# Threshold attention and a gated feed-forward on one core: second pair's transposes, value loads and weight loads moved later in the opening slots, idle transposes added on TensorE

## The chip, the cores and the metric

The kernel runs on one core of one Trainium2 chip. The metric is the device time of a whole execution in microseconds (us). Six runs of the kernel before gave a median of 565.81 us (563.64 to 567.03). A further execution was recorded by the hardware profiler; every duration of a single instruction below comes from that one.

## The reference

Two stages, for 8 batches of 8 heads with 576 positions of 64 values each:

```python
# stage 1, for every batch and head
scores = q @ k.T / 8
thresh = max(scores, axis=-1) - tau                # tau = 0.02
scores = where(scores >= thresh, scores, -1e9)
attn   = exp(scores - max(scores))
attn   = attn / (sum(attn) + 1e-9)
y      = attn @ v
# stage 2; x is y with heads side by side: 4608 tokens of 512
h   = x @ w_in                                     # 512 -> 2048
g   = h * clip(h + 3, 0, 6) / 6
out = g @ w_out                                    # 2048 -> 512, float32
```

## The kernel before

**Units of work.** A *pair* is two heads of a batch; a *quad* is two pairs. There are 16 quads, two for each batch. For each quad the main loop (L439) runs 9 *slots*, 144 in all; n counts them from 0. Slots 0 to 3 of a quad are the four blocks of 128 query rows of its first pair, slots 4 to 7 those of its second pair, and slot 8 takes the last 64 rows of all four heads. Each slot is two tiles (one per head) of 128 rows by 576 keys.

**A slot's softmax** runs over four engines. TensorE (PE) computes the scores into PSUM (`scores`, L251); VectorE (DVE) copies each tile to SBUF and takes the row maximum (`sm_max`, L271); GpSimd (POOL) turns the maximum into a bias (L281); ScalarE (ACT) masks by the threshold (`sm_mask`, L284) and, one slot later, exponentiates (`sm_exp`, L289); DVE inverts the row sums (L293); POOL scales and writes bf16 (`sm_norm`, L296). The result must then be transposed. In most slots SP issues a DMA transpose (L307). In every second slot of the first `N1` = 22 (the flag `on_chip`, L434) PE does it two slots later with nine transposes into the one buffer of pool `ps_h` (`pe_transpose`, L310), and DVE copies it out (L316).

**Inputs.** `load_quad` (L80) makes five load jobs for a quad: keys of the first pair, queries of the first pair, the 64 left-over rows, keys of the second pair, queries of the second pair. Each job is two DMAs from SP (queries of the last batches are four). `load_v` makes four POOL DMAs per batch, `load_weights` sixteen for `w_in` and sixteen for `w_out`, also from POOL, which casts them to bf16 on the way. `start(jobs, n)` issues the next n jobs of a list; the loop does this at the end of every slot (L515 to L517). q and k must be transposed before use: `transpose_q`, `transpose_k` (four PE transposes of 128x128 each, L214, then one copy) and `transpose_rest` (L229).

**Order.** The program is in the order in which it is written: each engine runs its own instructions strictly in this order and waits for the others by semaphores. So an instruction that waits holds back all that stands behind it on its engine. `scores` for slot n+1 are issued at the end of slot n (L510), after the transposes of slot n. The pool of score tiles `ps_s` has two buffers, so the scores of slot n+1 wait for `sm_max` of slot n. `ps_h` has one buffer: the on-chip transposes and the hidden layer of stage 2 (`mm1`, L349) take turns in it.

**Opening.** Five load jobs of quad 0 are issued, fourteen idle transposes of the identity (`warm_up`, L163) run on PE, the first pair is transposed with four more idle ones between, and `transpose_rest(0)` copies its pieces out: two copies of keys through `copy_out` (ACT ahead of slot 0 and from slot `N1` on, DVE between), then one copy of queries by DVE (L242). POOL waits at L426 for the transposed keys (a copy of one column into `gate`) and then issues the four value loads of batch 0. The second pair of quad 0 is transposed in slots 1 (queries) and 2 (keys). After slots 0 to 3 two weight loads each are issued, later one per slot; quad 1's loads go two jobs per slot.

**Stage 2.** From slot 23 on each slot but the last of a quad also runs one item of `mm1` (two blocks of hidden units), `mm1_relu` on ACT or DVE, `mm1_gate` on DVE, and later four matmuls of `mm2_part`. `av_main` and `av_rest` multiply by the values.

Of the kernel before, what the change touches and what calls it, by code (L numbers as in the profile page):

```python
# [9 lines left out]
F32 = mybir.dt.float32  # L10
# [5 lines left out]
P = 128  # L16
# [5 lines left out]
def kernel(  # L22
# [10 lines left out]
    nc = tc.nc  # L33
    B, H, S, D = q.shape
# [8 lines left out]
    N1 = 22  # L43
# [4 lines left out]
    singles = ctx.enter_context(tc.tile_pool(name="singles", bufs=1))  # L48
# [12 lines left out]
    ps_s = ctx.enter_context(tc.psum_pool(name="ps_s", bufs=2))  # L61
    ps_h = ctx.enter_context(tc.psum_pool(name="ps_h", bufs=1))
# [11 lines left out]
    loads = []  # L74
    casts = []
    vcasts = []
# [39 lines left out]
    def load_v(b):  # L116
        vm = v_pool.tile([P, H, 4 * D], BF16, tag="vm", name="vm")
        vr = vrs[b % 2]
        vsb[b] = (vm, vr)
        for g in range(2):  # L120
            vcasts.append(lambda g=g: nc.gpsimd.dma_start(
                out=vm[:, g * 4:g * 4 + 4, :],
                in_=v[b, g * 4:g * 4 + 4, 0:512, :].rearrange("h (p t) d -> p h (t d)", t=4)))
        for a in range(2):
            vcasts.append(lambda a=a: nc.gpsimd.dma_start(
                out=vr[a * 64:(a + 1) * 64, a, :, :],
                in_=v[b, :, 512:S, :].rearrange("(hp a) p d -> a p hp d", a=2)[a]))
# [21 lines left out]
    def start(jobs, n):  # L149
        for _ in range(min(n, len(jobs))):  # L150
            jobs.pop(0)()
# [6 lines left out]
    identf = singles.tile([P, P], F32)  # L158
    make_identity(nc, identf)

    warm = ps_s.tile([P, 2, 512], F32, tag="s", name="warm")

    def warm_up(count):  # L163
        for _ in range(count):
            nc.tensor.transpose(warm[:, 0, 0:P], identf[:], identf[:])

# [12 lines left out]
    def alloc_qk(quad):  # L179
        qkT[quad] = (qk_pool.tile([P, 2, S], F32, tag="qT", name="qT"),  # L180
                     qk_pool.tile([P, 2, S + 64], F32, tag="kT", name="kT"))

    def qT_of(pair):
        return qkT[pair // 2][0][:, pair % 2, :]

    def kT_of(pair):
        return qkT[pair // 2][1][:, pair % 2, :]
# [4 lines left out]
    def bank(name):  # L192
        nonlocal turn
        turn += 1
        if now < N2 and turn % 2:
            return ps_o.tile([P, 512], F32, tag="o", name=name)
        return ps_m.tile([P, 512], F32, tag="m", name=name)


    def copy_out(out, in_):  # L200
        if 0 <= now < N1:
            nc.vector.tensor_copy(out=out, in_=in_)
        else:
            nc.scalar.copy(out=out, in_=in_)  # L204


    def by_pe(pair):
        return pair // NPAIR < NB
# [16 lines left out]
    def transpose_k(pair):  # L225
        ps = main_pe(nat[pair // 2][1], pair)
        return lambda: copy_out(kT_of(pair)[:, 64:576], ps[:])

    def transpose_rest(quad):  # L229
        ps = bank("tr")  # L230
        nq, _, kr = nat[quad]
        nc.tensor.transpose(ps[:, 0:P], kr[:], identf[:])
        if by_pe(2 * quad):
            nc.tensor.transpose(ps[:, P:2 * P], nq[:, 1024:1152], identf[:])

        def evict():
            qT, kT = qkT[quad]
            both = ps[:].rearrange("p (w n t) -> p w n t", n=2, t=64)
            copy_out(kT[0:64, :, S:S + 64], both[0:64, 0])
            copy_out(kT[64:P, :, 0:64], both[64:P, 0])  # L240
            if by_pe(2 * quad):
                nc.vector.tensor_copy(out=qT[:, :, 512:S], in_=both[:, 1])  # L242
        return evict

    def keys(pair, a, hf):
        kT = kT_of(pair)
        c0 = 64 * (1 - a) + hf * HALF
        return kT[a * 64:(a + 1) * 64, c0:c0 + HALF]


    def scores(quad, slot):  # L251
        tiles = [ps_s.tile([P, 2, 512], F32, tag="s", name="s") for _ in range(2)]
        for hf in range(2):
            if slot < 8:
                pair, t = 2 * quad + slot // 4, slot % 4
                for a in range(2):
                    nc.tensor.matmul(tiles[a][:, hf, 0:HALF], qT_of(pair)[a * 64:(a + 1) * 64, t * P:(t + 1) * P],  # L257
                                     keys(pair, a, hf), start=True, stop=True)
            else:
                for n in range(2):  # L260
                    for a in range(2):
                        pair = 2 * quad + n
                        nc.tensor.matmul(tiles[a][n * 64:(n + 1) * 64, hf, 0:HALF],  # L263
                                         qT_of(pair)[a * 64:(a + 1) * 64, 512:S], keys(pair, a, hf),
                                         start=True, stop=True)
        return tiles
# [22 lines left out]
    def sm_exp(sl, i):  # L289
        s = sl.s[:, i, :]  # L290
        nc.scalar.activation(out=s, in_=s, func=Act.Exp, accum_out=sl.rsum[:, i:i + 1])  # L291
# [123 lines left out]
        return items  # L415

    alloc_qk(0)
    gate = singles.tile([P, 1], F32)
    evict = transpose_k(0)
    warm_up(4)  # L420
    evict_q = transpose_q(0)
# [1 line left out]
    evict_q()  # L423
    transpose_rest(0)()

    nc.gpsimd.tensor_copy(out=gate[:], in_=kT_of(0)[:, 64:65])  # L426
    start(vcasts, 4)

    queue = []
    for quad in range(NQUAD):  # L430
        for slot in range(NSLOT):
            sl = Slot()
            sl.quad, sl.slot = quad, slot
            sl.on_chip = len(queue) < N1 and len(queue) % 2 == 1  # L434
            queue.append(sl)
    queue[0].tiles = scores(0, 0)

# [1 line left out]
    for n, sl in enumerate(queue):  # L439
        quad, slot = sl.quad, sl.slot  # L440
        b, g = divmod(quad, 2)
        now = n
        if slot in (0, 4):
            pts[2 * quad + slot // 4] = pt_pool.tile([P, 9, 512], BF16, tag="pT", name="pT")
        if slot == 8:
            ptr[quad] = ptr_pool.tile([P, 9, P], BF16, tag="pR", name="pR")
        if quad == 0 and slot == 0:
            load_quad(1)
        if slot == (4 if quad else 8) and quad + 2 < NQUAD:
            load_quad(quad + 2)  # L450
        if slot == 0 and g == 1 and b + 1 < B:
            load_v(b + 1)
        if prev is not None:
            for i in range(2):
                sm_exp(prev, i)
        sm_max(sl)

        if slot != 8 and todo1:
            item, then = todo1.pop(0)
            h = mm1(item)  # L460
            r = mm1_relu(h, on_act=(slot in (0, 1, 3, 5)))
            mm1_gate(item, h, r)
            todo2.extend(then)
        copies = pe_transpose(queue[n - 2]) if n > 1 and queue[n - 2].on_chip else None
        if prev is not None:
            sm_recip(prev)
        if copies:
            copies()
        outs = []


        pieces = 0 if slot == 3 else 1
        if slot == 0:
            second = True
        if second and slot < 2 and len(todo2) > 1 and todo2[0][1] == todo2[1][1]:
            pieces, second = 2, False
        for _ in range(pieces):
            if todo2:
                bb, mt, part = todo2.pop(0)
                mm2_part(bb, mt, part)  # L480
                if part == 3:
                    outs += mm2_out(bb, mt, on_act=False)
        for i in range(2):
            sm_mask(sl, i)
        evict = None
        nxt = 2 * quad + 2
        if slot == 1:
            evict = transpose_q(2 * quad + 1)
        elif slot == 2:
            evict = transpose_k(2 * quad + 1)  # L490
        elif slot == 3 and quad > 0:
            av_main(2 * quad - 1)
        elif slot == 4 and quad > 0:
            av_rest(quad - 1)
            if quad % 2 == 0:
                todo1.extend(moe_of(quad // 2 - 1))
        elif slot in (5, 6, 7) and quad + 1 < NQUAD:
            if slot == 5:
                alloc_qk(quad + 1)
                evict = transpose_q(nxt)  # L500
            elif slot == 6:
                evict = transpose_k(nxt)
            else:
                evict = transpose_rest(quad + 1)
        elif slot == 8:
            av_main(2 * quad)
        if evict:
            evict()
        if n + 1 < len(queue):
            queue[n + 1].tiles = scores(queue[n + 1].quad, queue[n + 1].slot)  # L510
        if prev is not None:
            sm_norm(prev)
        flush()
        late.extend(outs)
        start(loads, 2 if n < 3 else 1)  # L515
        start(vcasts, 1 if n > 12 else 0)
        start(casts, 2 if n < 4 else 1)  # L517
        prev = sl

    for i in range(2):  # L520
# [66 lines left out]
```

## Time and profile before

| what | value |
|---|---|
| median of 6 runs | 565.81 us (563.64 to 567.03) |
| the profiled execution's own time | 564.15 us |
| its span, first to last instruction | 562.4 us |
| PE busy (matmul) | 528.3 us, 94% |
| ACT busy | 469.4 us, 83% |
| DVE busy | 425.3 us, 76% |
| POOL busy | 305.5 us, 54% |
| one fp32 score matmul, 64x288 | 436 ns mean, 1024 of them |
| one mask / one exponential on ACT | 766 / 671 ns |
| one row-maximum pass on DVE | 751 ns |
| one normalising pass on POOL | 745 ns |

Busy time on PE overlaps itself, because matmuls are pipelined. A line of the timeline gives: start in us from the span's first instruction, length in us, engine, line of the program, operation, output<-input, shape, and xN for N instructions of the same kind run together. In brackets stands how long the engine had been idle, and what released it. A line of the windows view gives, for one stretch of time, its length, the busy time of PE, PE's weight loads, DVE, ACT and POOL (with counts), the granted TensorE clock as a fraction of full speed, the busy share of the DMA engines, and GB/s.

### The profile page before, as it was taken

To read this page: it belongs to the slowest core of one execution; us is meant where nothing else is said; L and a number is where in the kernel's file an instruction comes from. 1 tells how busy PE (TensorE), PEld (TensorE's weight loads), DVE (VectorE), ACT (ScalarE), POOL (GpSimd) and SP (SyncE) were. 2 spreads that over 40 slices of the span, in tenths; PEclk is the share of its full clock that TensorE was granted. 3 is DMA by queue.
4 is the path that set the end of the run, shared out by engine and by line. 5 is a ranking of instruction groups with operands and counts; after the bars stand their busy time and mean duration, and the time that the engine had idled before them with its cause. 6 is when DMAs were issued, how large, how long until landed. Compare 5 with 4: busy or idle time off the path is not lost.

```text
span 562.4 us, 11515 instructions
## 1 busy us (share of the span) xinstructions
PE 528.3 (94%) x3776; PEld 305.1 (54%) x3817; DVE 425.3 (76%) x1041; ACT 469.4 (83%) x999; POOL 305.5 (54%) x647
## 2 busy tenths in 40 slices
PE   6798788999999999999999999999999999999996
PEld 4454445655545555555555565655555555654653
DVE  3588777797878788787878798887878798883540
ACT  4699896998988999989898999899898999983540
POOL 4788875654556556655456655655556555561000
PEclk9899998999999999999999999999999999999999
DMA  7999989977589877977589788987789965653102
GB/s 125 174 135 162 192 140 142 149 130 155 122 150 148 155 151 148 175 145 162 107 145 179 150 149 149 182 147 147 125 144 169 158 135 120 99 105 89 38 20 75
DMA packets 285020, 77.22 MB, mean 137 GB/s; under 512 B 268064, under 2 KB 280352, under 8 KB 284960
## 3 DMA queue, kind: packets, MB, share of 16 engines
q1 hardware_dynamic: 267552, 67.57, 66.0%
q0 software_dynamic: 17408, 8.92, 13.8%
q8 instruction: 30, 0.49, 0.4%
q14 instruction: 30, 0.25, 0.1%
HBM read 36.70 MB, written 9.44 MB: 82 GB/s over the span
## 4 chain that ended last, share of the span: by engine, by line
PE 61%; DVE 11%; ACT 6%; issue 3%; DMA 1%; SPq 1%; POOL 1%; DVEq 0%
PE h L354 18%; PE o L383 18%; PE s L257 17%; DVE s L278 5%; PE av L324 4%; DVE g L371 3%; ACT s L286 2%; DVE r L365 2%; ACT s L291 2%; ACT r L363 2%; PE s L263 1%; PE tp L214 1%; DMA nq<-in_q_dram 1%; PE av L327 1%; PE ar L324 1%
## 5 line engine op out<-in xcount | busy, mean ns | idle before, releaser
L299 POOL TENSOR_SCALAR pn<-s,rinv 128x576 bf16<-128x576 f32 x288 | 211.6, 745 | 136.4 <-DVE rinv L294 60.3
L286 ACT ACTIVATE s<-s,bias 128x576 f32<-128x576 f32 x288 | 206.8, 766 | 36.4 <-POOL bias L281 35.1
L278 DVE TENSOR_SCALAR_CACHE_REDUCE s<-s 128x576 f32<-128x576 f32 x288 | 205.9, 751 | 40.2 <-PE s L257 31.9
L291 ACT ACTIVATE s<-s 128x576 f32<-128x576 f32 x288 | 192.7, 671 | 0.3
L257 PE MATMUL s<-kT,qT 64*128 64x288 f32 x1024 | 173.2, 436 | 5.9 <-DVE s L278 5.8
L354 PE MATMUL h<-xT,w_in_sb 128*128 128x320 bf16 (+1 forms) x1024 | 146.1, 288 | 4.5 <-DVE g L371 3.5
L383 PE MATMUL o<-w_out_sb,g 128*128 128x512 bf16 x535 | 133.5, 379 | 5.6 <-DVE osb L391 2.7
L354 PEld LDWEIGHTS <-w_in_sb 128*128 128x128 bf16 x1024 | 92.4, 98 | 68.7 <-issue 30.9
L257 PEld LDWEIGHTS s<-kT,qT 64*128 64x128 f32 x1024 | 95.5, 189 | 62.7 <-DVE s L278 27.6
L371 DVE SCALAR_TENSOR_TENSOR g<-r,h 128x512 bf16<-128x512 f32 (+1 forms) x128 | 96.3, 754 | 39.5 <-ACT r L363 37.5
L281 POOL TENSOR_SCALAR bias<-m 128x1 f32<-128x1 f32 x288 | 54.4, 189 | 60.8 <-DVE s L278 41.5
L383 PEld LDWEIGHTS <-g 128*128 128x128 bf16 x576 | 55.5, 98 | 57.9 <-issue 9.5
L363 ACT ACTIVATE r<-h,three 128x640 f32<-128x640 f32 (+1 forms) x74 | 54.4, 737 | 22.4 <-PE h L354 21.7
L291 ACT ACTIVATION_READ_ACCUMULATOR s<-s 128x1 f32 x288 | 54.2, 188 | 0.0
L365 DVE TENSOR_SCALAR r<-h 128x512 f32<-128x512 f32 (+1 forms) x54 | 40.5, 750 | 0.0
L391 DVE TENSOR_SCALAR osb<-o 128x512 f32<-128x512 f32 x31 | 20.9, 676 | 22.2 <-PE o L383 22.2
L324 PE MATMUL av<-pT,vm 128*64 128x512 bf16 x256 | 33.7, 385 | 0.3 <-ACT kT L204 0.3
L294 DVE RECIPROCAL rinv<-rsum 128x2 f32<-128x2 f32 x144 | 22.9, 159 | 11.4 <-ACT s L291 10.4
L324 PEld LDWEIGHTS <-vm 128*64 128x64 bf16 x512 | 17.9, 110 | 23.4 <-issue 16.4
L336 DVE CAST xT<-av 128x512 bf16<-128x512 f32 x32 | 21.7, 679 | 4.8 <-PE av L327 4.5
L278 DVE DVE_READ_ACCUMULATOR s<-s 128x1 f32 x288 | 23.8, 83 | 0.0
L389 ACT ACTIVATE osb<-o 128x512 f32<-128x512 f32 x5 | 3.0, 597 | 23.9 <-PE o L383 23.9
(43 smaller groups left out, 245.9 us busy)
## 6 DMA issues: line engine op xcount, KB each, us to landing
km<-in_k_dram SPq DMA_DIRECT2D x64, 128.0 KB, 3.1
out_dram<-osb SPq DMA_DIRECT2D x32, 256.0 KB, 2.4
nq<-in_q_dram SPq DMA_DIRECT2D x96, 72.0 KB, 2.8
vm<-in_v_dram POOLq DMA_DIRECT2D x16, 256.0 KB, 5.6
nq<-in_q_dram SPq DMA_DIRECT2D x16, 128.0 KB, 4.6
w_in_sb<-in_moe_w_in_dram POOLq DMA_DIRECT2D x16, 128.0 KB, 4.5
w_out_sb<-in_moe_w_out_dram POOLq DMA_DIRECT2D x16, 128.0 KB, 3.5
pT<-pn SPq DMA_TRANSPOSE x118, 3.5
```

The lines of the kernel that those rows point to most:

```text
L257: nc.tensor.matmul(tiles[a][:, hf, 0:HALF], qT_of(pair)[a * 64:(a + 1) * 64, t * P:(t + 1) * P], keys(pair, a, hf), start=True, stop=True)
L278: nc.vector.tensor_scalar(out=sl.s[:, i, :].rearrange("p (a b) -> p a b", a=2), in0=ps[:, :, 0:HALF], scalar1=1.0, scalar2=None, op0=Alu.m ...
L281: nc.gpsimd.tensor_scalar(out=sl.bias[:, i:i + 1], in0=sl.m[:, i:i + 1], scalar1=-scale, scalar2=tau, op0=Alu.mult, op1=Alu.add)
L286: nc.scalar.activation(out=s, in_=s, func=Act.Prelu, bias=sl.bias[:, i:i + 1], scale=scale, alpha=REJECT)
L291: nc.scalar.activation(out=s, in_=s, func=Act.Exp, accum_out=sl.rsum[:, i:i + 1])
L299: nc.gpsimd.tensor_scalar(out=pn[:, i, :], in0=sl.s[:, i, :], scalar1=sl.rinv[:, i:i + 1], scalar2=1.0, op0=Alu.mult, op1=Alu.mult)
L324: nc.tensor.matmul(ps[a * 64:(a + 1) * 64, :], vm[:, 2 * hp + a, c * D:(c + 1) * D], pT[:, 5 * a + c, cols], start=(c == 0), stop=False)
L354: nc.tensor.matmul(hps[:, n, 0:w], w_in_sb[:, ki, (ni + n) * P:(ni + n + 1) * P], xT[b][:, ki, c0:c0 + w], start=(ki == 0), stop=(ki == KI ...
L363: nc.scalar.activation(out=r, in_=hps, func=Act.Relu, bias=three[:])
L365: nc.vector.tensor_scalar(out=r, in0=hps, scalar1=3.0, scalar2=0.0, op0=Alu.add, op1=Alu.max)
L371: nc.vector.scalar_tensor_tensor(out=gbuf[:, ni:ni + 2, c0:c0 + w], in0=r, scalar=6.0, in1=hps, op0=Alu.min, op1=Alu.mult)
L383: nc.tensor.matmul(o_ps[0], gbuf[:, ni, mt * P:(mt + 1) * P], w_out_sb[:, ni, :], start=(ni == 0), stop=(ni == NI - 1))
```

## The change

- `warm_up` takes a tile of its own from `ps_h` (before: one tile of `ps_s`, taken once). After the scores of each of slots 0 to 7 it is called for six more idle transposes.
- In `transpose_rest` the queries' copy stands ahead of the two key copies.
- The second pair of quad 0 is transposed in slots 2 and 3 (before: 1 and 2). Other quads stay.
- `gate` and its copy are gone. The four value loads of batch 0 are issued one after each of slots 0 to 3.
- Weight loads begin after slot 4, one per slot, and from slot 24 on two per slot. (Before: two after each of slots 0 to 3, then one.)
- Input loads of quad 1 are one job per slot (before: two in slots 0 to 2).
- `on_chip` ends one slot earlier: slot 21 goes through a DMA transpose, so the PE transposes and the copy that stood in slot 23 are gone.

```diff
-    warm = ps_s.tile([P, 2, 512], F32, tag="s", name="warm")
-
     def warm_up(count):
+        warm = ps_h.tile([P, 2, 512], F32, tag="h", name="warm")
         for _ in range(count):
             nc.tensor.transpose(warm[:, 0, 0:P], identf[:], identf[:])
...
             both = ps[:].rearrange("p (w n t) -> p w n t", n=2, t=64)
+            if by_pe(2 * quad):
+                nc.vector.tensor_copy(out=qT[:, :, 512:S], in_=both[:, 1])
             copy_out(kT[0:64, :, S:S + 64], both[0:64, 0])
             copy_out(kT[64:P, :, 0:64], both[64:P, 0])
-            if by_pe(2 * quad):
-                nc.vector.tensor_copy(out=qT[:, :, 512:S], in_=both[:, 1])
...
-    gate = singles.tile([P, 1], F32)
...
-    nc.gpsimd.tensor_copy(out=gate[:], in_=kT_of(0)[:, 64:65])
-    start(vcasts, 4)
-
...
-            sl.on_chip = len(queue) < N1 and len(queue) % 2 == 1
+            sl.on_chip = len(queue) < N1 - 1 and len(queue) % 2 == 1
...
-        if slot == 1:
+        if slot == (1 if quad else 2):
             evict = transpose_q(2 * quad + 1)
-        elif slot == 2:
+        elif slot == (2 if quad else 3):
             evict = transpose_k(2 * quad + 1)
...
             queue[n + 1].tiles = scores(queue[n + 1].quad, queue[n + 1].slot)
+        if n < 8:
+            warm_up(6)
         if prev is not None:
             sm_norm(prev)
         flush()
         late.extend(outs)
-        start(loads, 2 if n < 3 else 1)
-        start(vcasts, 1 if n > 12 else 0)
-        start(casts, 2 if n < 4 else 1)
+        start(loads, 1)
+        if n < 4 or n > 12:
+            start(vcasts, 1)
+        if n > 3:
+            start(casts, 1 if n < 24 else 2)
```

## The prediction

> **What bounds the kernel now.** I read the chain of waits first. PE is 61% of it, but the chain ends its way back at 78.33 us: of the first 78 us it says nothing. Then the stages: from 100 to 540 us PE is busy 430 of 440 us at clock 1.00. The change touches nothing there except four POOL issues in slots 28 and 29, so it is a change of the first 110 us, and what it gains there shifts the rest. These first 110 us I read in the timeline, by the starts of the masks on ACT, one pair per slot.
>
> ```profile
> 5.42 0.62 PE L165 MATMUL warm<-identf 128*128 128x128 f32 x4
> ...
> 13.22 1.42 ACT L286 ACTIVATE s<-s,bias 128x576 f32<-128x576 f32 x2
> ...
> 15.27 0.70 PE L214 MATMUL tp<-identf,nq 128*128 128x128 f32 x4 [3.08 <-DMA nq<-in_q_dram]
> ...
> 15.89 2.29 PE L257 MATMUL s<-kT,qT 64*128 64x288 f32 x8
> ...
> 19.29 1.45 ACT L286 ACTIVATE s<-s,bias 128x576 f32<-128x576 f32 x2 [3.32 <-POOL bias L281]
> ...
> 22.87 1.44 ACT L286 ACTIVATE s<-s,bias 128x576 f32<-128x576 f32 x2 [0.79 <-POOL bias L281]
> ```
>
> Slot 1 masks at 13.22, slot 2 at 19.29: 6.07 us, where a slot's ACT work is two masks and two exponentials, 2.68 us start to start. The cause stands between: PE sat 3.08 us in front of the second pair's query transposes until their load landed, and the scores of slot 2 stood behind them. After the idle time these took 2.29 us; 28.73 us shows the same eight at 1.24. The page names POOL for the 3.32 us, but POOL waited for DVE and DVE for PE. Slots 3 and 4 come 0.79 and 0.40 us late, because POOL issues two weight loads (1.13 us) ahead of the bias. From there to slot 21 ACT repeats every 2.7 to 3.4 us. The second place is slots 23 to 27:
>
> ```profile
> 82.17 0.69 DVE L371 SCALAR_TENSOR_TENSOR g<-r,h 128x512 bf16<-128x512 f32 x1 [0.79 <-ACT r L363]
> ...
> 82.91 0.66 PE L315 MATMUL pt<-identb,pn 128*128 128x128 bf16 x9 [1.64 <-DVE g L371]
> ...
> 86.37 1.45 ACT L286 ACTIVATE s<-s,bias 128x576 f32<-128x576 f32 x2 [1.59 <-POOL bias L281]
> ...
> 92.52 0.29 DVE L242 COPY qT<-tr 128x128 f32<-128x128 f32 x1 [1.64 <-ACT kT L204]
> ...
> 93.53 3.02 PE L257 MATMUL s<-kT,qT 64*128 64x288 f32 x8 [1.61 <-DVE s L278]
> ```
>
> In slot 23 the on-chip transposes wait 1.64 us for the single `ps_h` buffer, which the first hidden tile holds until its gate. In slot 25 DVE waits 1.64 us for ACT's key copies, and PE behind it 1.61.
>
> ```profile
> 92.00:94.00 2.00, 0.47 (x2) 0.29 (x2) 1.49 (x4) 1.96 (x8) 1.20 (x3) 1.00 1.37 231
> 94.00:100.00 6.00, 5.98 (x24) 3.42 (x22) 3.12 (x10) 4.19 (x9) 2.55 (x6) 0.52 1.10 188
> ```
>
> After that pause the granted clock is 0.52 for 6 us.
>
> **The opening, step by step.** Start shift: with the queries' copy first, ACT's two key copies wait for it: 0.29 us and a hand-over, so scores, maximum and mask of slot 0 come 0.34 later (mask 10.88), slot 1 at 13.56. The `gate` copy (0.18 us) and the four value issues (1.70 and 1.26 us, ended 9.36) leave POOL before its first bias at 10.31: they were hidden. The loads they competed with are not: the late queries were issued at 7.33 and landed at 15.27, with 0.6 MB of values (two of 256 KB, two of 32) ahead. Now they share the queues with input loads alone, and are wanted only at about 15.3, behind slot 2's start. I take that wait as gone; if it is not, up to 3.08 us return.
>
> Then I step on with the rows' durations: eight scores 1.24 us, row maxima 0.67 each start to start, reciprocal 0.08, copy of a transposed tile 0.65, eviction 0.60, normalising 1.47, bias 0.2, value issue 0.80 or 0.66, weight issue 0.58. Six idle transposes: four took 0.62 with a last latency of 0.27, so 0.117 each, 0.70 for six, and with the 0.17 gap that PE shows between kinds 0.87.
>
> - Slot 2: scores of slot 2 follow slot 1's maxima at once. Mask limited by POOL (normalise 13.95 to 15.42, value issue to 16.2, bias): **16.5**, was 19.29.
> - Slot 3: one value issue (0.80) stands where two weight issues stood; **19.2**, was 22.87.
> - Slot 4: the new wait. The keys of the second pair are now evicted in slot 3 and used at its end. Exponential of slot 2 ends 19.25, reciprocal, copy and eviction to 20.7, scores of slot 4, their maximum from 22.05, bias, mask **23.1** (was 26.04). ACT was ready at 21.9: 1.2 us of the gain goes here.
> - Slot 5 **26.25** (28.71), slot 6 **28.9** (31.46), slot 7 **31.75** (34.27), slot 8 **34.45** (36.95). PE's sequence in the fullest, slot 5: transposes 0.55, pair transposes 0.54, scores 1.0 without their last latency, idle ones 0.87: 2.96 against ACT's 2.68; slots 6 and 7 have 2.4 and 2.8. The idle ones also wait in `ps_h` for slot n's copy by DVE in slots 3, 5, 7, with the next slot's transposes, evictions and scores behind them. But that copy stands ahead of the next slot's maxima anyway, and by this walk they end before the next scores may start.
>
> Gain carried out of the opening: **2.5 us**. Below: 0.5 if the idle transposes bind in most slots. Above: 3.5 if slot 4's wait is hidden.
>
> Moved loads: quad 1's jobs come in slots 0 to 4, the first queries now behind slot 0's DMA transpose on SP (about 15.4); they are wanted at about 25.8, median landing is 5.2 us in this stage. Values issued from 11.6 to 21.7, wanted at slot 8 (34). Sixteen `w_in` loads are out after slot 19, the first wanted at 80 us. These cost nothing.
>
> **Slots 21 to 30**, on the old clock. Nine transposes (0.66) and a copy (0.76) leave slot 23; one DMA transpose joins SP with four slots until its use. DVE goes from the reciprocal (82.77) through the queries' eviction to slot 24's maxima at 83.45 instead of 85.29. Mask of 24: 85.47 (86.37), held by POOL. From slot 24 two weight issues per slot: POOL needs normalise 1.47, issues 1.16, biases 0.46, 3.1 us. Mask 25: 89.35 (90.62). In slot 25 the queries' copy no longer waits for ACT (1.64 us); ACT itself sets slot 26: 92.65 (93.85). PE's longest pause there falls from 1.61 to about 0.8 us, so I expect the clock to hold: 27 at 95.97 (99.00), a lead of 3. In slots 27 to 29 value issues come on top: 1.47 + 0.46 + 0.80 + 1.08 = 3.8 us per slot on POOL, where slots 28 and 29 took 2.9 and 3.7. That gives most back: 28 at 100.65 (103.20), 29 at 104.65 (106.09), 30 at 108.5 (109.81). Gain: **1.3 us**. Bounds: 0.3 (clock falls again and POOL binds) and 2.6 (POOL's extra issues hide).
>
> [...]
>
> **Sum.** 2.5 + 1.3 = 3.8 us off the profiled execution's 564.15: 560.35. That execution lies 1.66 below the median of the runs, so **562.0**.
>
> **Rivals.**
> 1. *Idle transposes bind (slower).* Place: PE in slots 0 to 7, pool `ps_h`. If each six stands wholly on the path, 0.87 x 8 = 7.0 us against 3.8 gained: 569.0. From 0.48 us per slot uncovered the whole gain is gone. For it: slot 5's PE sequence exceeds ACT's period, and each six waits for DVE in every second slot. Against: PE was busy only 2.41 of 4 us from 24 to 28. At half clock it would be worse. 13%.
> 2. *Given back (no change).* Opening gain 1.2 (slot 4's wait larger, POOL late), middle 0.3: 564.3. For it: ACT, POOL and DVE all have periods near 2.7 us, so any extra wait is paid. Against: 3.3 us of idle ACT is a large thing to fill. 22%. That the idle transposes change no clock at all belongs here and costs nothing more.
> 3. *All of it stays.* Slot 4 hidden, clock held, POOL's doubled issues under slots that are limited elsewhere: 3.5 + 2.6: 559.7. 15%.
>
> The forecast has 50%. A measurement tells about 0.3% (1.7 us) from no change. Faster: the forecast nearly whole and rival 3, 0.64; within: 0.23; slower: 0.13. Range: from rival 3 with 1 us more, 558.5, to rival 2 with the lower part of rival 1, 566.0.
>
> **What would show it.** Mask starts of slots 2, 4 and 8 at 16.5, 23.1 and 34.5; no DMA wait before the second pair's transposes; an ACT wait of about 1 us in slot 4; no idle PE time before scores that a block of idle transposes ends; no stage at clock 0.5 about 90 us; POOL full in slots 27 to 29. Wrong, if the lead at slot 8 is under 1 us (then PE's order binds), or if it is there and gone by slot 31.

## The result, and the profile after

| | before | after |
|---|---|---|
| median | 565.53 us (36 runs, 563.04 to 567.72) | 562.12 us (17 runs, 561.05 to 565.45) |
| ratio, 95% interval | | 0.9947 (0.9933 to 0.9960) |
| the profiled execution's own time | 564.15 us | 562.81 us |
| its span | 562.4 us | 561.0 us |
| mean granted clock over the runs whose clock is on record | 0.987 (98 runs, those beside the experiments) | 0.995 (17 runs) |

The change makes the kernel 0.5% faster: 3.0 us by the ratio, 2.3 to 3.8 by its interval. The two profiled executions are only 1.34 us apart; why, the rest of this document asks too.

First the timeline of the kernel after (columns as before: start, length, engine, line, operation), at the places that answer to those shown of before:

```profile
13.47 1.43 ACT L285 ACTIVATE s<-s,bias 128x576 f32<-128x576 f32 x2
...
14.66 0.88 PE L164 MATMUL warm<-identf 128*128 128x128 f32 x6
...
15.38 0.60 PE L213 MATMUL tp<-identf,nq 128*128 128x128 f32 x4
...
16.37 1.44 ACT L285 ACTIVATE s<-s,bias 128x576 f32<-128x576 f32 x2
...
19.07 1.44 ACT L285 ACTIVATE s<-s,bias 128x576 f32<-128x576 f32 x2
...
20.64 1.24 PE L256 MATMUL s<-kT,qT 64*128 64x288 f32 x8 [1.51 <-DVE kT L201]
...
23.08 1.45 ACT L285 ACTIVATE s<-s,bias 128x576 f32<-128x576 f32 x2 [1.25 <-POOL bias L280]
```

The query transposes at 15.38 have no bracket: the DMA wait of 3.08 us is gone, and slot 2 masks at 16.37 (before 19.29). In slot 4 a new wait stands: PE waits 1.51 us for the second pair's keys, which are evicted in the slot that uses them, and ACT 1.25 us behind it. The bracket says POOL; POOL waited for DVE's maxima, and these for PE.

Then the later places, from the timeline of the kernel after:

```profile
69.72 1.47 POOL L298 TENSOR_SCALAR pn<-s,rinv 128x576 bf16<-128x576 f32 x2 [1.33 <-DMA pT<-pn]
...
72.01 1.44 ACT L285 ACTIVATE s<-s,bias 128x576 f32<-128x576 f32 x2 [1.09 <-POOL bias L280]
...
90.46 1.23 PE L256 MATMUL s<-kT,qT 64*128 64x288 f32 x6 [0.47 <-ACT kT L203]
...
99.87 1.44 ACT L285 ACTIVATE s<-s,bias 128x576 f32<-128x576 f32 x2 [1.40 <-POOL bias L280]
...
103.79 1.44 ACT L285 ACTIVATE s<-s,bias 128x576 f32<-128x576 f32 x2 [1.15 <-POOL bias L280]
...
105.75 1.92 PE L323 MATMUL av<-pT,vm 128*64 128x512 bf16 x8 [2.04 <-ACT kT L203]
```

Slot 20 loses time where the forecast saw none: POOL cannot write `pn` again before a DMA transpose has read it (1.33 us at 69.72). ACT's wait of 1.40 us at 99.87 is explained by the timeline of POOL alone:

```profile
97.71 0.80 POOL L121 DMA_DIRECT2D vm<-in_v_dram  x1
98.51 1.07 POOL L146 DMA_DIRECT2D w_out_sb<-in_moe_w_out_dram  x2
99.65 0.46 POOL L280 TENSOR_SCALAR bias<-m 128x1 f32<-128x1 f32 x2
100.21 1.47 POOL L298 TENSOR_SCALAR pn<-s,rinv 128x576 bf16<-128x576 f32 x2
```

Its lines follow each other almost without a gap: value issue, two weight issues, only then the bias for which ACT waits, and the next normalising pass. The same sequence stands ahead of the 1.15 us at 103.79. In before, with one weight issue there, the mask of the same slot waited half as long:

```profile
103.20 1.44 ACT L286 ACTIVATE s<-s,bias 128x576 f32<-128x576 f32 x2 [0.67 <-POOL bias L281]
```

The windows of the same execution show the clock (columns: window, length, busy time of PE, its weight loads, DVE, ACT, POOL, then granted clock, DMA share, GB/s):

```profile
92.00:94.00 2.00, 1.29 (x9) 0.65 (x6) 2.00 (x6) 2.00 (x5) 1.77 (x3) 1.00 1.24 221
94.00:96.00 2.00, 1.29 (x7) 0.77 (x7) 0.73 (x4) 1.98 (x5) 1.13 (x4) 1.00 1.29 133
...
104.00:106.00 2.00, 0.25 (x2) 0.18 (x3) 0.22 (x2) 2.00 (x4) 1.91 (x4) 0.82 1.34 176
106.00:108.00 2.00, 2.00 (x10) 0.68 (x6) 0.35 (x1) 2.00 (x6) 1.66 (x5) 0.50 1.39 198
```

At 94 us, where before fell to half clock (0.55 from 94 to 96 us), it holds at 1.00. Towards the end of the pause of 2.04 us that ends at 105.75 it falls to 0.50.

So the gain has a course. The lead over before, by the start of the first mask of a slot:

| slot | 2 | 4 | 8 | 19 | 20 | 22 | 24 | 27 | 30 | 32 | 35 | 48 |
|---|---|---|---|---|---|---|---|---|---|---|---|---|
| lead, us | 2.92 | 2.96 | 2.11 | 1.72 | 0.53 | 0.75 | 1.64 | 3.86 | 2.23 | 1.72 | 1.47 | 1.49 |

It falls twice, from slot 8 to 20 and from 27 to 35, and 1.47 us of the 3.86 at slot 27 is left. From there to the end little changes (the spans are 1.4 apart).

### The profile page after: what moved, and what is told of

Its sections match the earlier page's. It is cut to its first block, busy times and chain, and to the rows that moved or that the text cites. A ratio compares the mean times of both kernels' runs of the same rounds, so it can differ in the third digit from the quotient of the medians.

```text
span 561.0 us, 11593 instructions
## 1 busy us (share of the span) xinstructions
PE 530.6 (95%) x3815; PEld 308.6 (55%) x3856; DVE 424.1 (76%) x1040; ACT 470.2 (84%) x999; POOL 305.8 (55%) x646
## 4 chain that ended last, share of the span: by engine, by line
PE 61%; DVE 11%; ACT 7%; issue 3%; SPq 1%; DMA 1%; POOL 1%; DVEq 0%; POOLq 0%
PE h L353 18%; PE o L382 18%; PE s L256 17%; DVE s L277 4%; PE av L323 4%; ACT s L285 3%; DVE g L370 2%; ACT s L290 2%; DVE r L364 2%; ACT r L362 2%; PE s L262 1%; DMA nq<-in_q_dram 1%; PE tp L213 1%; PE ar L323 1%; PE av L326 1%
## 5 line engine op out<-in xcount | busy, mean ns | idle before, releaser
L256 PE MATMUL s<-kT,qT 64*128 64x288 f32 x1024 | 170.9, 431 | 5.9 <-DVE s L277 3.2
L256 PEld LDWEIGHTS s<-kT,qT 64*128 64x128 f32 x1024 | 94.1, 186 | 62.7 <-DVE s L277 24.9
```

## The experiments

Each kernel was timed beside before on the same chip, and the ratio is to that before; the chips differ from one experiment to another, so kernels are better compared by ratio than by median. The stages are differences of mask starts in the profiled execution, one for each kernel.

| kernel | median, us | ratio (95%) | slots 4 to 8 | 8 to 22 | 22 to 34 |
|---|---|---|---|---|---|
| before | | 1 | 10.91 | 41.69 | 44.67 |
| after | 562.12 | 0.9947 (0.9933–0.9960) | 11.76 | 43.05 | 43.71 |
| e1: after, no idle transposes | 563.00 | 0.9957 (0.9943–0.9971) | 13.75 | 41.56 | 43.20 |
| e2: after, single weight issues to slot 30 | 566.89 | 1.0017 (1.0000–1.0033) | 11.76 | 44.39 | 42.77 |
| e3: after, second pair in slots 1, 2 | 561.28 | 0.9935 (0.9916–0.9954) | 11.51 | 43.45 | 43.21 |
| e4: before, loads moved only | 562.99 | 0.9952 (0.9938–0.9965) | 10.93 | 41.76 | 47.64 |
| e5: after, old copy order | 562.50 | 0.9942 (0.9923–0.9961) | 12.14 | 42.28 | 44.38 |
| e6: after, slot 21 on PE again | 565.16 | 0.9987 (0.9970–1.0004) | 11.77 | 43.43 | 45.86 |
| e7: before, copy order and slot 21 only | 561.40 | 0.9928 (0.9909–0.9947) | 12.55 | 41.57 | 40.99 |
| e8: after, double issues in slots 22 to 26 only | 561.73 | 0.9931 (0.9910–0.9952) | 11.77 | 44.04 | 42.63 |
| e10: loads moved, slot 21, double issues in 22 to 26 | 559.45 | 0.9891 (0.9857–0.9926) | 10.94 | 41.75 | 44.17 |
| e11: e10 with the idle transposes | 560.39 | 0.9908 (0.9878–0.9938) | 11.80 | 42.21 | 44.20 |
| e12: e10 with the new copy order | 557.90 | 0.9880 (0.9863–0.9897) | 10.91 | 41.63 | 42.62 |
| e13: e10 once more, beside e12 | 558.77 | 0.9892 (0.9873–0.9912) | 10.91 | 41.68 | 43.27 |

### The opening: loads, slots of the second pair

**e4** is before with the moved loads alone:

```diff
-    gate = singles.tile([P, 1], F32)
...
-    nc.gpsimd.tensor_copy(out=gate[:], in_=kT_of(0)[:, 64:65])
-    start(vcasts, 4)
...
-        start(vcasts, 1 if n > 12 else 0)
-        start(casts, 2 if n < 4 else 1)
+        if n < 4 or n > 12:
+            start(vcasts, 1)
+        if n > 3:
+            start(casts, 1 if n < 24 else 2)
```

> The kernel before with one part of the change: no gate, value loads one per slot in slots 0 to 3, weight loads from slot 4 on, two per slot from slot 24 on. Theory (the loads alone remove the 3.08 us wait): slot 2's mask at about 16.4 instead of 19.29, slot 4 at about 21.9, slot 8 at about 33.5 (before 36.95); of this lead of 3.4 us about 1 is lost in slots 20 to 30, time about 563. Rival (the move to slots 2 and 3 is needed): slot 2's mask at 18 or later, lead at slot 8 under 1.5 us, time 564.5 or more.

The timeline of e4 has no wait ahead of the query transposes, and an early slot 2:

```profile
12.01 0.66 PE L214 MATMUL tp<-identf,nq 128*128 128x128 f32 x4
...
16.03 1.44 ACT L286 ACTIVATE s<-s,bias 128x576 f32<-128x576 f32 x2 [0.15 <-POOL bias L281]
```

Which loads held the queries up is in the DMA view from 8.0 to 11.2 us, ahead of before's first weight issue at 11.23 (q0 are POOL's loads, q1 those of SP; packets, MB, share of the engines; the last line ends with the time to landing). First before, then e4:

```profile
q0 software_dynamic: 492, 0.25, 67.5%
q1 hardware_dynamic: 668, 0.17, 32.4%
...
nq<-in_q_dram SPq DMA_DIRECT2D x2, 128.0 KB, 7.3
```

```profile
q1 hardware_dynamic: 2729, 0.68, 93.7%
...
nq<-in_q_dram SPq DMA_DIRECT2D x3, 128.0 KB, 2.7
```

In before POOL's queue, with nothing but values in it yet, took 0.25 MB, and SP moved 0.17 MB where e4 moved 0.68. What the weight loads from 11.23 on added to the landing at about 15.1 was not separated.

Slot 8 came at 32.39: a lead of 4.56 us, over twice that of the whole change (2.11). So the opening's gain is that of the loads alone, and the other edits of the opening take half of it back. Of this lead 3 us are lost later: slots 22 to 34 take 47.64 us (before 44.67), with slot 21 still on PE, double issues, and half clock twice (0.50 to 0.51 from 90 to 96 us, 0.50 from 108 to 110).

**e3** puts the second pair back into slots 1 and 2 of the changed kernel:

```diff
-        if slot == (1 if quad else 2):
+        if slot == 1:
...
-        elif slot == (2 if quad else 3):
+        elif slot == 2:
```

> The changed kernel with the second pair of quad 0 transposed in slots 1 and 2 again. Theory (the early value loads made the queries land late; without them they land before 13.5 us): no wait, or under 0.5 us, before these transposes, slot 2's mask within 0.3 us of 16.37, slot 4's mask at about 22.0 instead of 23.08 since the keys are no longer evicted and used in the same slot, time 1 us below the changed kernel. Rival (the queries land at about 15 whatever the values do, and the later slot is what hides it): a DMA wait of 1 us or more in slot 1, slot 2's mask at 18 or later, time 1.5 to 2.5 us above the changed kernel.

The timeline of e3 on PE shows what was asked:

```profile
13.47 1.54 PE L164 MATMUL warm<-identf 128*128 128x128 f32 x6
14.80 1.06 PE L213 MATMUL tp<-identf,nq 128*128 128x128 f32 x4
```

The queries were there when PE came to them, at 14.80, one slot earlier than in the changed kernel. So the loads ahead of them had delayed them, and shifting the pair was not needed. Its profiled execution ran at clock 0.50 to 0.72 from 10 to 18 us (six idle transposes 1.54 us, not 0.87); the fall began before the first idle transposes of its slots, and its opening stages are no measure. The median is 0.84 us below the change's, with overlapping intervals.

What the shift costs is plainest between two kernels with early loads and idle transposes. In e11, with the pair in slots 1 and 2, slot 4 follows slot 3 after 2.74 us (18.85, 21.59); in the changed kernel after 4.01 (19.07, 23.08). That is 1.27 us, the wait of 1.25 at 23.08. With 0.24 from the start shift and 0.86 from the idle transposes (below) this makes 2.4 us, what e4's lead at slot 8 has over the change's.

### The idle transposes

**e1** leaves them out of slots 0 to 7:

```diff
-        if n < 8:
-            warm_up(6)
```

> The changed kernel without the six idle transposes in slots 0 to 7. Theory (they change no clock and cost PE only a little): clock 1.00 through slots 1 to 8 as in the changed kernel (masks of slots 2, 4, 8 at 16.4, 23.1, 34.8 there), masks of slots 2 and 4 within 0.2 us of these, slot 8 earlier by 0.3 to 0.5 us, because slots 6 and 7 took 2.9 to 3.0 us where ACT needs 2.68; time 561 to 562.5. Rival one (they hold the clock up): a stage at half clock in slots 1 to 5, slot 4 at least 1 us later, time 563.5 or more. Rival two (they bind on PE): slot 8 earlier by over 1 us, time about 560.5.

The windows of e1:

```profile
12.00:16.00 4.00, 3.95 (x14) 2.34 (x10) 1.73 (x6) 3.74 (x10) 2.13 (x5) 0.50 0.50 66
16.00:20.00 4.00, 3.82 (x27) 2.26 (x25) 3.30 (x9) 3.50 (x9) 3.38 (x8) 0.81 0.59 73
20.00:24.00 4.00, 1.61 (x12) 0.82 (x10) 2.59 (x8) 2.77 (x6) 2.49 (x6) 1.00 1.19 189
24.00:28.00 4.00, 4.00 (x19) 2.57 (x20) 2.23 (x9) 3.58 (x8) 2.70 (x7) 0.55 1.01 162
28.00:32.00 4.00, 3.76 (x17) 2.15 (x15) 2.30 (x5) 2.08 (x5) 2.03 (x4) 0.60 0.75 102
```

The first half-clock stretch began at 10.7 us (clock 0.68 from 10 to 12 us, 0.50 from 12 to 16), ahead of the place of the first idle transposes (12.36 in the changed kernel), so their absence did not cause it. The second is the one that the changed kernel does not have: here PE was busy 1.61 of 4 us from 20 to 24, where slot 4 waits for the late keys, and then the clock was at half for 6.8 us; there PE was busy 3.22 of the same 4 us, and the clock is 1.00 from 20 to 32. My theory that they change no clock fell, though this execution had the lowest mean clock of e1's eleven runs (0.986; their mean is 0.992, that of the change 0.995). And part of the loss came back: slots 8 to 22 took 41.56 us against 43.05, and the medians are 0.9 us apart with overlapping intervals.

**e10 and e11** try them where PE has no such pause: loads moved, pair in slots 1 and 2, old copy order. e10's edits against before are those of e4, the last line replaced, and the one of slot 21:

```diff
-            sl.on_chip = len(queue) < N1 and len(queue) % 2 == 1
+            sl.on_chip = len(queue) < N1 - 1 and len(queue) % 2 == 1
...
+            start(casts, 2 if 21 < n < 27 else 1)
```

> This joins the two parts that carried a gain alone: the moved loads (values in slots 0 to 3 without the gate, weights from slot 4) and slot 21 by DMA transpose, with double weight issues only in slots 22 to 26; the second pair stays in slots 1 and 2, no idle transposes, old copy order. Theory (the two gains have different places and add where POOL's late double issues don't take the second back): mask 2 at 16.0, mask 8 at 32.4, slots 0 to 22 in 63.7 us, slots 22 to 34 in 42.6 as in the run with double issues in 22 to 26, so a lead of 6 us over before at slot 34 and 559.5 us. Rival (the two are alternatives: what comes early waits later for the same loads or falls to half clock): slots 22 to 34 take 46 us or more and the time is 562 or above.

e11 adds `warm_up(6)` in slots 0 to 7 again, with its tile from `ps_h`.

> The same kernel with the six idle transposes in each of slots 0 to 7, as the change has them. Theory (idle transposes hold the clock in slots 4 to 11 but cost the lead on the way): slots 4 to 8 take 11.7 us with them against 10.9 without, slots 8 to 22 take 42.3 to 44.4 against 41.7, and the time is 0.5 to 2 us above the run without them. Rival (they pay by the clock): the clock of the run without them falls to 0.5 to 0.6 about slots 5 to 11 and the time with them is 1 us or more below it.

The windows of e10, without idle transposes:

```profile
20.00:24.00 4.00, 2.81 (x19) 1.70 (x20) 2.84 (x9) 4.00 (x10) 3.73 (x8) 1.00 1.07 184
24.00:28.00 4.00, 3.57 (x23) 2.19 (x22) 3.44 (x9) 3.99 (x10) 3.18 (x8) 1.00 0.79 128
28.00:32.00 4.00, 3.71 (x41) 1.70 (x38) 3.52 (x10) 3.98 (x10) 3.73 (x8) 1.00 1.00 124
```

and of e11, with them:

```profile
20.00:24.00 4.00, 3.82 (x27) 2.53 (x26) 3.06 (x9) 4.00 (x10) 3.68 (x7) 1.00 1.11 187
24.00:28.00 4.00, 4.00 (x35) 3.02 (x33) 3.27 (x9) 3.85 (x10) 2.80 (x9) 1.00 0.90 131
28.00:32.00 4.00, 3.94 (x42) 2.54 (x39) 3.40 (x10) 3.76 (x9) 3.74 (x7) 1.00 0.82 123
```

The clock is 1.00 in both. With idle transposes PE is busy 4.00 and 3.94 of 4 us and sets the pace; ACT, full in e10 (3.99), has idle time. Slots 4 to 8 take 0.86 us more. The rest of the theory held too, nearly: 0.94 us in the median (intervals overlap), and slots 8 to 22 at 42.21 against 41.75. The second gain did add to the first, against the rival; only slots 22 to 34 took 44.17, not 42.6, with clock 0.62 from 88 to 92 us. That led to e12.

### The middle: slot 21, the copy order

**e7** is before with the two edits of the middle alone, `N1 - 1` and the queries' copy first.

> The kernel before with only the two edits of the middle: queries' copy first, slot 21 by DMA transpose. Weight loads stay one per slot, so POOL does not bind in slots 28 to 30. Theory: opening as before but 0.3 us later (slot 2 at 19.6), from slot 23 on a lead that reaches 2 to 3 us at slot 27 and stays at 1.5 to 2.5 us at slot 31 (before 113.32), no half clock after slot 26; time about 563.5. Rival (the lead of the middle is lost whatever POOL does): lead at slot 31 under 0.5 us, time 565 or more.

Slots 22 to 34 in 40.99 us instead of 44.67, and a time 3.0 to 5.1 us below before by its interval: more than I expected. It is no slower than the whole change (intervals overlap), though it leaves the late queries' wait (2.61 us) where it was. With single weight issues nothing is given back in slots 27 to 30 (10.76 us; the change 12.44). **e6** takes the slot-21 edit back out of the changed kernel (`N1` again):

> The changed kernel with slot 21 transposed on PE again. Theory: PE waits about 1.6 us for the one buffer in slot 23, mask of slot 24 later than 84.73 by 0.9 to 1.5 us relative to slot 23, slot 30 later by 0.5 or more; time 0.5 to 1.2 us above the changed kernel. Rival (given back by POOL in slots 27 to 30): slot 30 within 0.3 us, time equal.

The timeline of e6 shows the wait of before again, and ACT's behind it:

```profile
82.52 0.66 PE L314 MATMUL pt<-identb,pn 128*128 128x128 bf16 x9 [1.64 <-DVE g L370]
...
85.99 1.45 ACT L285 ACTIVATE s<-s,bias 128x576 f32<-128x576 f32 x2 [1.59 <-POOL bias L280]
```

Slots 22 to 34 take 2.15 us more than in the changed kernel, and no gain over before can be told (0.9987, the interval includes 1): I had expected a loss of 0.5 to 1.2 us. By the ratios this one edit carries about three quarters of what the change brings.

**e5** puts the key copies ahead of the queries' copy again.

> The changed kernel with the old order of copies in the left-over rows (keys by ACT first, then queries by DVE). Theory (the order frees DVE from ACT in slot 25): DVE waits about 1.6 us for ACT's key copies in slot 25, mask of slot 27 later than 95.14 by 1 us or more, slot 30 by 0.5 or more, half clock after slot 26; in the opening slot 0's mask 0.3 us earlier; time 0.5 to 1.2 us above the changed kernel. Rival (POOL sets slots 27 to 30 anyway): slot 30 within 0.3 us of 107.58, time equal or 0.3 us lower.

No difference in the median: the rival held. But its profile shows a pause of 2.16 us on PE ahead of the scores of slot 27 (which are issued in slot 26), where the changed kernel has 0.47, and half clock after it (0.50 from 94 to 96 us), and so does e10's (0.50 from 90 to 92). **e12** therefore adds the new order to e10, and **e13** is e10 again beside it:

```diff
+            if by_pe(2 * quad):
+                nc.vector.tensor_copy(out=qT[:, :, 512:S], in_=both[:, 1])
             copy_out(kT[0:64, :, S:S + 64], both[0:64, 0])
             copy_out(kT[64:P, :, 0:64], both[64:P, 0])
-            if by_pe(2 * quad):
-                nc.vector.tensor_copy(out=qT[:, :, 512:S], in_=both[:, 1])
```

> The moved loads, slot 21 by DMA transpose and double weight issues in slots 22 to 26, and now the queries' copy ahead of the key copies. Theory (the copy order takes away the pause of PE in front of slot 26's scores and with it the half clock after it): the pause there falls from 2.16 us to about 0.5, the clock stays at 1.00 from 84 to 96 us, slots 22 to 27 take 16.7 to 17.3 us (18.75 with the old order), and the time is 0.5 to 1.5 us below that of the old order, near 558.5, less 0.24 us that the new order costs at the start. Rival (as in the run of the change with the old order, nothing comes through to the end): slots 22 to 27 shorter, but slots 22 to 34 within 0.5 us of 44.2, and the two times equal.

> The same kernel with the old copy order, once more, beside the former on the same chip. If the first look told its nature: 559.5 us, half clock near 90 us behind a pause of 2.16 us on PE, slots 22 to 34 in 44.2 us. If that was chance: no such pause, and slots 22 to 27 near 17 us.

PE ahead of the same scores, in e10:

```profile
87.89 2.73 PE L257 MATMUL s<-kT,qT 64*128 64x288 f32 x8 [2.16 <-DVE s L278]
```

and in e12:

```profile
86.06 2.06 PE L257 MATMUL s<-kT,qT 64*128 64x288 f32 x8 [0.32 <-DVE s L278]
```

Both lines are the scores of slot 27 (the expectation calls it the pause ahead of slot 26's). The pause went from 2.16 to 0.32 us, as the theory has it, and slots 22 to 27 from 18.75 to 17.25. But e13, the same kernel as e10, paused 2.14 us and kept clock 1.00: slots 22 to 27 in 17.37, and of the expected 559.5 us it took 558.77. So the copy order certainly removes a pause; the half clock came after that pause in e10's execution and not in e13's. The medians of e12 and e13 are 0.87 us apart in the expected direction, with overlapping intervals. e12 is the best kernel of this study: 1.2% below before (1.0 to 1.4%), all four runs between 557.88 and 558.65.

### The weight issues

**e2** issues one weight load per slot to slot 30:

> The changed kernel with one weight load per slot up to slot 30, and two from slot 31 on (before: two from slot 24 on). Theory (the second weight issue makes POOL late in slots 27 to 30, which gave back half of the middle gain and made PE wait 2.04 us for ACT's key copy in slot 30, with the clock at half for 4 us after it): masks of slots 28, 29, 30 earlier than 99.87, 103.79, 107.58 by 0.5, 1.0, 1.3 us or more, no half clock near 107 us, time 1.0 to 1.5 us below the changed kernel, about 561. Rival (the lead is lost to ACT and DVE there anyway): slot 31 within 0.4 us of 111.04 and the time the same.

It is slower than before by the median, with an interval that just reaches 1, and no gain of the change is left. Its profiled execution is the slowest of its 22. The relief came as expected (slots 27 to 30 in 11.32 us instead of 12.44), and then the timeline of PE shows the price:

```profile
122.08 0.38 PE L382 MATMUL o<-w_out_sb,g 128*128 128x512 bf16 x1 [0.85 <-DMA w_out_sb<-in_moe_w_out_dram]
123.94 0.38 PE L382 MATMUL o<-w_out_sb,g 128*128 128x512 bf16 x1 [1.49 <-DMA w_out_sb<-in_moe_w_out_dram]
126.02 0.58 PE L382 MATMUL o<-w_out_sb,g 128*128 128x512 bf16 x1 [1.70 <-DMA w_out_sb<-in_moe_w_out_dram]
```

The second matmul needs the last `w_out` blocks in slot 34, and slot 35 came 8.21 us after slot 34 (3.25 in before). Who starts weights at slot 4 must catch up somewhere: the double issues pay for the early values. **e8** catches up in slots 22 to 26, before the values come on top (`2 if 21 < n < 27 else 1`):

> The changed kernel with the two weight loads per slot in slots 22 to 26 only, one elsewhere, so that the last is issued in slot 30 and slots 27 to 29 carry one beside the value load. Theory (POOL's second issue beside the value loads costs 1 us between slots 27 and 30): from slot 27 to slot 30 11.3 us or less where the changed kernel took 12.44, PE's wait of 2.04 us in slot 30 under 1 us, no half clock near 107 us, no wait for weights before the second product; lead at slot 31 larger by 0.8 us or more; time about 1 us below the changed kernel. Rival (lost again to other engines by slot 34): slot 34 within 0.4 us of 121.60, time equal.

Slots 27 to 30 took 11.30 us, 22 to 34 1.08 us less than in the changed kernel, and no half clock near 107 (1.00 from 104 to 116 us). Its execution lost 2.37 us to the DMA transpose at slot 20 instead, so the lead at slot 31 (1.73) was not larger. By medians it is 0.4 us below the change, within the intervals.

## Why the prediction was right

The forecast was 562.0, the median is 562.12. The direction and most steps stand. That the number fits this well is luck: two errors cancel.

- **Load wait "taken as gone"**: right. No wait at 15.38, and e3 and e4 show that the moved loads had made it.
- **The walk to slot 5**: 16.5, 19.2, 23.1, 26.25 were foreseen; 16.37, 19.07, 23.08, 26.13 came. The start shift was 0.24, not 0.34. The new wait of slot 4 (1.2 foreseen) is 1.25.
- **Idle transposes "end before the next scores may start"**: this step failed, mildly. Six took 0.87 us as worked out, but slots 6 to 8 came at 29.07, 32.09, 34.84 (28.9, 31.75, 34.45 foreseen). e11 against e10: 0.86 us in four slots. The first rival's mechanism is real, at an eighth of its 7.0 us in these slots. Lead at slot 8: 2.11, not 2.5.
- **The idle transposes and the clock**: one execution of before has clock 1.00 from 20 to 94 us without them, and I took that for what every execution shows there. That was wrong. e1 and e7, both without them, fell to half clock at 24.4 and 26.2 us; the changed kernel has 1.00 from 20 to 32. In slots 1 and 2 they come too late for the early falls that were seen: e1's at 10.7 and e3's at 10.9 us, where the first idle transposes run at 12.36 in the change and at 13.47 in e3. And e1's second fall follows the pause that the shifted pair makes (1.45 us up to 21.72): with early loads and the pair in its old place e4, e10, e12 and e13 have 1.00 from 20 to 32 us without idle transposes.
- **Slots 8 to 21 as neutral**: wrong, and the largest miss. The lead falls from 2.11 to 0.75 us, 1.19 of it from slot 19 to 20. "These cost nothing" was said of the moved loads. Yet e4, e10, e12 and e13 move the same loads and take 41.63 to 41.76 us from 8 to 22. All seven kernels with idle transposes take 42.21 to 44.39, all seven without 41.56 to 41.76. So the loss comes with the idle transposes, not with the loads. In e8 the clock even was 0.64 from 68 to 72 us, and in e6 0.96 over 36 to 80 us. Over these 44 us it was 1.00 in the changed kernel, e5 and e11, and without idle transposes in before, e1, e4, e7 and e10.
- **Slots 21 to 30**: gain 1.3 foreseen; the lead grew from 0.75 at slot 22 to 2.23 at slot 30, 1.48. To slot 27 it grew by 3.11 (3.03 foreseen), and POOL full in 27 to 29 took 1.63 back (1.72). PE's longest pause there was 0.73 us (0.8 foreseen). e6 and e7 show that the slot-21 edit carries this stage.
- **After slot 30, nothing**: wrong by 0.76. The half clock at 106 (0.50 from 106 to 108 us) and the slots behind it took the lead from 2.23 to 1.47.
- **Sum and offset**: foreseen 560.35 for the profiled execution, measured 562.81: the three misses 0.4, 1.36 and 0.76 make 2.5. The offset to the median was taken as +1.66 from before; after's execution lies 0.69 above its median, so this term was off by 2.35 the other way. These errors cancel. The offset goes in part with the clock: over the 98 runs of before whose clock is on record, a run takes 2.8 us more for each 0.01 less of mean clock, and the change lifts the mean from 0.987 to 0.995, by this slope 2.3 us. The profiled execution of before had 0.990, which stands for 0.8 us less than at its mean. That of after had 0.995, its mean, so its 0.69 is not explained by this. The slope is a correlation: a pause of PE costs time by itself, half clock followed the one ahead of slot 27's scores in four of six executions (last section), and no run separates the two.

Of the rivals, "given back" describes the profiled pair (1.34 us) better than the forecast does; the medians are the forecast's.

## What to carry to other kernels

When a load arrives late, take away what it queues behind before moving the work that needs it: here the first did all, and the second cost 1.25 us. Filling PE's idle time to hold its clock shortened a stage here only where PE paused (slots 4 to 8: 11.76 us in the change, 13.75 in e1); where it did not, it cost 0.86 us (e11 against e10). So look first whether another edit removes the pause. And do not carry an offset between one profiled execution and a median over a change that alters the mean clock (here from 0.987 to 0.995).

## What the runs showed that I had not expected

**A pause and the clock.** In the six kernels with the old copy order PE paused 1.61 to 2.16 us in the same place, ahead of the scores of slot 27. Four executions fell to half clock after it (0.50 from 96 to 100 us in before, from 92 to 96 in e4, from 94 to 96 in e5, from 90 to 92 in e10), two did not (e11 and e13, 1.00 from 84 to 96). With the new order (at most 0.5 us there, 0.7 in the slot after) none of eight did at that place; e6 fell one slot later, at 98.0 us (0.51 from 98 to 100). Here are the windows around the pause, in e10, where it ends at 87.89:

```profile
84.00:86.00 2.00, 1.73 (x21) 0.50 (x13) 0.77 (x2) 1.99 (x6) 1.74 (x5) 1.00 1.36 162
86.00:88.00 2.00, 0.11 (x1) 0.12 (x2) 1.13 (x4) 1.97 (x6) 1.92 (x5) 1.00 1.52 164
88.00:90.00 2.00, 1.98 (x8) 1.17 (x8) 1.31 (x5) 2.00 (x5) 1.42 (x4) 0.74 1.34 200
90.00:92.00 2.00, 2.00 (x9) 1.04 (x8) 1.40 (x4) 0.97 (x4) 1.80 (x5) 0.50 1.27 230
```

and in e13, the same kernel, where it ends at 87.51:

```profile
84.00:86.00 2.00, 1.37 (x14) 0.48 (x10) 0.41 (x2) 1.98 (x5) 1.74 (x5) 1.00 1.27 157
86.00:88.00 2.00, 0.49 (x2) 0.29 (x2) 1.51 (x4) 1.96 (x8) 1.64 (x4) 1.00 1.34 202
88.00:90.00 2.00, 1.98 (x14) 1.23 (x13) 1.63 (x7) 2.00 (x5) 1.68 (x4) 1.00 1.33 248
90.00:92.00 2.00, 1.90 (x13) 1.24 (x11) 1.28 (x4) 1.95 (x4) 1.41 (x4) 1.00 1.13 231
```

The pauses are 2.16 and 2.14 us long, so their length does not tell the two executions apart; before fell after 1.61 us, and e11 kept its clock after 2.16. What does tell them apart was not shown.

**DMA transposes and idle transposes.** Of those issued from 40 to 78 us the slowest DMA transpose took 10.7 to 11.4 us from issue to landing in each of the seven kernels with idle transposes, and 7.6 to 9.4 in each of the seven without. The DMA view of the changed kernel, from 61.0 to 64.5 and from 64.5 to 66.5 us (an issue line ends with its time to landing):

```profile
DMA packets 2159, 0.73 MB, mean 209 GB/s; under 512 B 1748, under 2 KB 2159, under 8 KB 2159
...
pT<-pn SPq DMA_TRANSPOSE x1, 11.0
...
DMA packets 247, 0.07 MB, mean 33 GB/s; under 512 B 239, under 2 KB 247, under 8 KB 247
```

For two us hardly anything moved (33 GB/s, after 209), though SP and POOL issued five transfers in them; the transpose landed at about 69.5, and POOL's `pn` started at 69.72. Such a lull (under 50 GB/s for 1.5 us or more) lies between 61 and 68 us in six of the seven kernels with idle transposes, all but e2, and there is none in before, e1, e4, e7 and e10, which have no idle transposes; before, e4, e7 and e10 have theirs after 72 us. Why idle transposes that ended 30 us before should shift them stays open: no run was made that separates it. Nor were the other losses of these kernels between slots 8 and 22 traced one by one.
